# A linear-attention and mixer kernel: VectorE's small product of u's and w's rows moves ahead of three products of the second unit

## Chip, cores and metric

The kernel runs on one core of a Trainium2 chip. A core has TensorE (PE, matrix products into PSUM; a weight load is shown as PEld), VectorE (DVE), ScalarE (ACT), GpSimd (POOL) and SyncE (SP), which run side by side, each through its own queue in order, and wait for one another by semaphores. Data comes from HBM into SBUF by DMAs that SP, ACT and GpSimd issue. The metric is device time in microseconds (us); the median of several runs is compared.

## What is computed

Two stages follow each other. The first is a linear attention with a decayed state (4 batches, 8 heads, 768 steps, 48 columns a head):

```python
for t in range(S):
    kt, vt, rt = (k[:, :, t], v[:, :, t], r[:, :, t])
    cur = np.einsum('bhd,bhe->bhde', u[None] * kt, vt)
    y[:, :, t] = np.einsum('bhd,bhde->bhe', rt, state + cur)
    state = w[None, :, :, None] * state + np.einsum('bhd,bhe->bhde', kt, vt)
```

The second is a mixer on x, which is y with the heads side by side (4 x 768 x 384):

```python
xt = x.transpose(0, 2, 1)
h = np.maximum(xt @ w_tok1, 0.0) @ w_tok2
u = x + h.transpose(0, 2, 1)
h2 = np.maximum(u @ w_ch1, 0.0) @ w_ch2
return (u + h2).astype(np.float32)
```

## The kernel before

The attention is worked in blocks of steps: scores between the steps of a block, masked to the causal half, and a state that carries what lies before the block. Powers of w are kept as tables (exp of iota times ln w); k and r are multiplied by them, turned by PE so that the columns lie on the partitions, and multiplied with each other to give scores (`at_ps`). The own step's term (u times k times r, summed over a head) comes apart from that: the product `pr` of the turned k and r goes through PE against `u_blk`, a matrix with u times w on its block diagonal, since the exponents of the two tables add up to -1 for the own step.

The first batch takes its 768 steps as three units of 256 (`pair_unit`): partition p holds steps 2p and 2p+1, so each of k and r is scaled in two steps (j = 0, 1). The other batches take 128 steps at a time (`unit`). The mixer of a batch follows its attention and overlaps the next batch's.

Nothing here is ordered by a scheduler at run time. The program makes 889 tasks, each with the tasks that it depends on, and emits them in the order of the list `ORDER`; `keep_in_program_order` holds every engine's instructions to that. The choice of engine of a flexible task (`flex`) is the list `ENGINES`, that of buffers the list `BUFS`. Two tasks on one engine therefore run in the order in which `ORDER` has them, and a task that waits holds up everything behind it on its engine.

The tasks around the change, by their number in `ORDER`:

- 126, 127: first unit's two products of k with its tables (GpSimd, VectorE). 130, 131: its two products of r (both VectorE). 128 and 132 turn them on PE; 129 and 133 copy the results to SBUF (`ka`, `rkb`) on ScalarE.
- 154, 155: second unit's products of k (both VectorE). 158, 159: its products of r (VectorE, GpSimd). 156 and 160 turn them on PE (`tk_ps`, `tr_ps`); 157 and 161 copy. 182: third unit's first product of k (GpSimd).
- 47: the small product `u_heads *= w_heads` on 8 partitions and 128 columns; both are parts of the tile `wp`, which the table of the same name fills later. It waits for the DMAs of u's and w's rows (issued by ACT at the start) and is on VectorE.
- 48: PE turns its result (`ud_ps`). 50: VectorE copies it onto the diagonal of `u_blk`. 139, 142: first unit's scores on PE; 140, 141, 143, 144: VectorE masks them (`AT`).
- 134: VectorE's product `pr` of the first unit; 135: PE's sum of it against `u_blk` (`ad_ps`).
- 43: GpSimd's `wGm` (a table of the state's decay). 61, 64, 67: GpSimd's loads of v for the three units. 119, 120: its loads of w_tok.
- 869 to 888: matmuls on zeros that keep PE warm (`kv_ps<-warm`).

VectorE's queue here is 127, 130, 131, 154, 155, 158, 47, 134, 50, 140, 143, 141, 144. PE's is 128, 132, 156, 48, 139, 142, 160, 135, with warming matmuls between. GpSimd's is 61, 64, 67, 159, 182, 43, 183, 119, 120.

Of the kernel before, what the change touches and what calls it, by code (L numbers as in the profile page):

```python
# [20 lines left out]
ORDER = [  # L21
    9, 57, 26, 3, 46, 0, 886, 884, 880, 1, 17, 8, 4, 6, 27, 24, 56, 59, 18, 19, 20, 10, 60, 2, 62, 878, 887,
    45, 42, 11, 12, 13, 21, 25, 14, 22, 63, 49, 877, 5, 29, 58, 65, 7, 16, 28, 23, 33, 126, 66, 31, 69, 888,
    34, 127, 869, 15, 68, 36, 32, 130, 131, 883, 30, 128, 61, 154, 129, 885, 132, 64, 133, 879, 155, 882,
    158, 67, 47, 134, 159, 156, 876, 48, 157, 50, 139, 140, 40, 142, 143, 160, 161, 182, 43, 141, 144, 135,
    873, 51, 52, 881, 170, 172, 872, 874, 71, 70, 38, 870, 162, 875, 186, 136, 35, 871, 145, 183, 184, 146,
    163, 119, 187, 171, 120, 73, 167, 138, 74, 147, 148, 185, 188, 150, 164, 149, 137, 173, 190, 191, 165,
    189, 151, 168, 121, 169, 166, 192, 152, 198, 199, 174, 175, 153, 195, 176, 197, 308, 178, 177, 179, 181,
# [1200 lines left out]
```

## Time and profile before

| what | us |
|---|---|
| three runs | 160.78, 165.18, 166.24 |
| median of them | 165.18 |
| profiled execution | 161.76 |
| its span, first to last instruction | 160.0 |
| loads of v, GpSimd: issue to landing, median of three | 8.2 |
| loads of k and r for the first batch's units, SP: issue to landing, median | 4.7 and 6.1 |

The profile is one execution; times in it count from the start of the span. Busy time of an engine leaves out register, semaphore and DMA-issuing instructions. "[1.23 <-DVE wp L274]" behind a row means that the engine sat idle for 1.23 us before it and that VectorE's write to wp ended that. All operations are recorded by one helper and so have the line L274; they are told apart by the tiles, out<-in. Recorded spans on GpSimd are rough.

### The profile page before, as it was taken

How to read it: one execution, taken by the hardware profiler on the slowest of the kernel's cores; microseconds unless marked ns; L12 is line 12 of the kernel's file. 1: busy time of each engine (PE TensorE's matmuls, PEld its weight loads, DVE VectorE, ACT ScalarE, POOL GpSimd, SP SyncE). 2: the span in 40 equal slices, each digit the busy share in tenths (PEclk: the TensorE clock that was granted, in tenths of full speed). 3: DMA queues.
4: the chain of work that ended last, by engine and by line, in shares of the span. 5: the costliest groups of instructions: out<-in, count | busy, mean ns of one | idle time of the engine just before them, and what ended most of it. 6: DMA issues, size and time to landing. Idle time of an engine off the chain costs nothing.

```text
span 160.0 us, 3938 instructions
## 1 busy us (share of the span) xinstructions
PE 153.3 (96%) x1563; PEld 102.3 (64%) x1564; DVE 116.1 (73%) x237; ACT 68.5 (43%) x154; POOL 77.7 (49%) x103
## 2 busy tenths in 40 slices
PE   6978999999999999999999999989999999999992
PEld 1455776777776666667767665656667556666662
DVE  5499895699697976697899888657998382644332
ACT  3874666649667263132852041168504202450100
POOL 7798569200899816955765543965906000000000
PEclk9999999999999999999999999999999999999999
DMA  4999999999999929999899899999794057010423
GB/s 124 263 243 183 165 195 222 222 205 181 197 196 214 200 74 217 211 228 212 153 196 222 157 200 187 178 210 209 148 189 103 4 158 185 2 49 4 147 74 123
DMA packets 88005, 26.60 MB, mean 166 GB/s; under 512 B 82738, under 2 KB 87092, under 8 KB 87988
## 3 DMA queue, kind: packets, MB, share of 16 engines
q1 hardware_dynamic: 82512, 22.52, 71.0%
q0 software_dynamic: 5280, 3.74, 15.2%
q8 instruction: 12, 0.20, 0.5%
q10 hardware_dynamic: 196, 0.11, 0.2%
q14 instruction: 5, 0.04, 0.1%
HBM read 20.46 MB, written 4.72 MB: 157 GB/s over the span
## 4 chain that ended last, share of the span: by engine, by line
PE 85%; DVE 6%; ACT 2%; DMA 2%; SPq 1%; issue 1%; DVEq 0%; ACTq 0%
PE h_ps L274 35%; PE z_ps L274 25%; PE y_ps L274 5%; PE kv_ps L274 5%; PE at_ps L274 4%; PE hT_ps L274 4%; DMA out_dram<-osb 2%; DVE kr L274 2%; PE hx_ps L274 2%; DVE wp L274 2%; SPq L274 1%; PE tr_ps L274 1%; PE w_ps L274 1%; PE trk L274 1%; DVE osb L274 1%
## 5 line engine op out<-in xcount | busy, mean ns | idle before, releaser
L274 PE MATMUL h_ps<-wch,zr 128*128 128x384 bf16 (+1 forms) x300 | 52.8, 320 | 0.0
L274 PE MATMUL z_ps<-uT,wch 128*128 128x384 bf16 x288 | 50.8, 326 | 0.2 <-DVE osb L274 0.2
L274 ACT ACTIVATE zr<-z_ps 128x384 bf16<-128x384 f32 x63 | 28.6, 492 | 41.4 <-PE z_ps L274 41.2
L274 PEld LDWEIGHTS <-wch 128*128 128x128 bf16 x288 | 31.5, 114 | 13.1 <-issue 0.7
L274 PEld LDWEIGHTS <-zr 128*128 128x128 bf16 x300 | 27.8, 98 | 16.1
L274 DVE TENSOR_SCALAR zr<-z_ps 128x384 bf16<-128x384 f32 x33 | 17.5, 553 | 10.1 <-PE z_ps L274 8.8
L274 DVE TENSOR_TENSOR AT<-at_ps,mask 128x512 bf16<-128x512 f32 x36 | 23.1, 682 | 0.9 <-PE at_ps L274 0.8
L274 DVE TENSOR_TENSOR osb<-u_sb,h_ps 128x384 f32<-128x384 bf16 (+1 forms) x19 | 10.1, 531 | 11.6 <-PE h_ps L274 7.8
L274 POOL TENSOR_TENSOR kr<-kt,wnat 128x384 bf16<-128x384 f32 x13 | 13.0, 1008 | 11.0 <-DMA kt<-in_k_dram 11.0
L274 POOL TENSOR_TENSOR yd<-vb,adg 128x384 f32<-128x384 bf16 x15 | 12.3, 829 | 8.0 <-ACT vb L274 7.4
L274 PEld LDWEIGHTS <-kr 128*128 128x128 bf16 (+1 forms) x196 | 12.4, 101 | 4.8 <-issue 2.0
L274 ACT CAST S<-kv_ps 48x192 bf16<-48x192 f32 (+1 forms) x26 | 8.8, 338 | 8.8 <-PE kv_ps L274 7.1
L274 POOL TENSOR_TENSOR rku<-ku,rt 128x384 f32<-128x384 f32 x10 | 10.2, 1019 | 3.1 <-DVE ku L274 1.8
L274 PEld LDWEIGHTS <-wtok 128*128 128x128 bf16 x84 | 8.0, 98 | 5.2
L274 POOL TENSOR_TENSOR ku<-kt,u_bc 128x384 f32<-128x384 f32 x10 | 9.9, 999 | 2.6 <-DVE rku L274 2.6
L274 DVE TENSOR_TENSOR x_b<-y_ps,yd 128x384 bf16<-128x384 f32 x18 | 9.7, 552 | 2.0 <-PE y_ps L274 1.8
L274 DVE TENSOR_TENSOR u_sb<-x_b,hT_ps 128x384 bf16<-128x384 bf16 x18 | 8.9, 550 | 2.7 <-PE hT_ps L274 2.6
L274 POOL TENSOR_TENSOR kr<-rt,wp 128x384 bf16<-128x384 f32 x9 | 9.1, 1009 | 3.5 <-ACT wp L274 3.5
L274 ACT CAST vb<-vt 128x384 bf16<-128x384 f32 x14 | 7.1, 514 | 6.2 <-DMA vt<-in_v_dram 6.1
L274 PE MATMUL kv_ps<-warm 128*128 128x512 bf16 x19 | 7.8, 521 | 1.5 <-DVE warm L274 1.5
L274 PE MATMUL h_ps<-x_b,wtok 128*128 128x384 bf16 x48 | 8.6, 326 | 0.0
L274 DVE TENSOR_REDUCE adg<-rku 128x8 f32<-128x384 f32 x12 | 6.6, 546 | 2.5 <-POOL rku L274 2.5
(108 smaller groups left out, 191.1 us busy)
## 6 DMA issues: line engine op xcount, KB each, us to landing
out_dram<-osb SPq DMA_DIRECT2D x23, 192.0 KB, 2.2
kt<-in_k_dram SPq DMA_DIRECT2D x18, 192.0 KB, 6.4
vt<-in_v_dram SPq DMA_DIRECT2D x18, 192.0 KB, 4.3
rt<-in_r_dram SPq DMA_DIRECT2D x12, 192.0 KB, 3.7
wch<-in_moe_w_ch_dram POOLq DMA_DIRECT2D x4, 384.0 KB, 7.5
zr<-in_k_dram SPq DMA_DIRECT2D x3, 384.0 KB, 4.7
zr<-in_r_dram SPq DMA_DIRECT2D x3, 384.0 KB, 6.1
win<-in_r_dram SPq DMA_DIRECT2D x3, 384.0 KB
```

The lines of the kernel that those rows point to most:

```text
L274: return lambda *args, **kw: tc.keep_in_program_order(f(*args, **kw))
```

## The change

Task 47 is emitted behind task 131, the second product of r of the first unit, and no longer behind task 158 (between 67 and 134). Since 130, 131, 154, 155 and 158 are VectorE's, as 47 is, its queue becomes 127, 130, 131, 47, 154, 155, 158, 134, 50 and so on. The tasks between the old and the new place on the other engines (883, 30, 128, 61, 129, 885, 132, 64, 133, 879, 882, 67 and the like) keep their order among themselves. The rest of the diff is the list's lines set anew.

```diff
-    34, 127, 869, 15, 68, 36, 32, 130, 131, 883, 30, 128, 61, 154, 129, 885, 132, 64, 133, 879, 155, 882,
-    158, 67, 47, 134, 159, 156, 876, 48, 157, 50, 139, 140, 40, 142, 143, 160, 161, 182, 43, 141, 144, 135,
+    34, 127, 869, 15, 68, 36, 32, 130, 131, 47, 883, 30, 128, 61, 154, 129, 885, 132, 64, 133, 879, 155,
+    882, 158, 67, 134, 159, 156, 876, 48, 157, 50, 139, 140, 40, 142, 143, 160, 161, 182, 43, 141, 144, 135,
```

The task itself is not touched:

```python
t_uw = flex({"DVE": "tiny_dve", "POOL": "tiny_pool"},
            lambda on: engine_of[on].tensor_mul(u_heads, u_heads, w_heads), [t_urows, t_wh])
```

## The prediction

> **What bounds the kernel now.** I read the page's head first, then busy time by stretch.
>
> ```profile
> span 160.0 us, 3938 instructions
> PE 153.3 (96%) x1563; PEld 102.3 (64%) x1564; DVE 116.1 (73%) x237; ACT 68.5 (43%) x154; POOL 77.7 (49%) x103
> 0.00:25.50 25.50, 22.35 (x328) 13.58 (x330) 20.91 (x49) 15.51 (x29) 19.61 (x40) 1.00 1.22 195
> 25.50:101.00 75.50, 75.46 (x797) 51.72 (x798) 61.14 (x123) 35.43 (x84) 43.84 (x49) 1.00 1.03 196
> 101.00:109.40 8.40, 7.77 (x56) 5.20 (x55) 4.94 (x10) 4.01 (x10) 5.97 (x7) 1.00 1.09 180
> 109.40:160.00 50.60, 47.71 (x386) 31.80 (x385) 29.08 (x57) 13.56 (x32) 8.27 (x9) 1.00 0.42 104
> ```
>
> In the stretches the columns are length, then busy us of PE, weight loads, VectorE, ScalarE, GpSimd, the granted TensorE clock (1.00 throughout), DMA share and GB/s. TensorE bounds the kernel: from 25.50 to 101.00 it lacks 0.04 us. Its idle time that an edit at the start can reach is in the first 25.5 us, and the small product is there. So the next view is the chain of waits around it (start, us, what).
>
> ```profile
> 6.72 2.99 DVE kr L274 x6
> 9.71 2.65 DVE wp L274
> 12.37 0.04 issue
> 12.41 0.38 PE ud_ps L274 x2
> ```
>
> The product of 8x128 numbers (wp<-wp) stands on the chain with 2.65 us behind VectorE's six products kr. The timeline of VectorE (start, duration) says that this is not its own cost:
>
> ```profile
> 7.20 0.64 DVE L274 TENSOR_TENSOR kr<-zr,wpair 128x384 bf16<-128x384 f32 x1
> 7.76 0.55 DVE L274 TENSOR_TENSOR kr<-zr,wpair 128x384 bf16<-128x384 f32 x1
> 8.23 0.54 DVE L274 TENSOR_TENSOR kr<-zr,u_sb 128x384 bf16<-128x384 f32 x1
> 8.70 0.55 DVE L274 TENSOR_TENSOR kr<-zr,u_sb 128x384 bf16<-128x384 f32 x1
> 9.17 0.54 DVE L274 TENSOR_TENSOR kr<-zr,wpair 128x384 bf16<-128x384 f32 x1
> 9.64 2.72 DVE L274 TENSOR_TENSOR wp<-wp 8x128 f32<-8x128 f32 x1
> 12.29 0.67 DVE L274 TENSOR_TENSOR pr<-tr_ps,ka 128x1024 bf16<-128x1024 bf16 x1
> 12.89 0.35 DVE L274 CAST u_blk<-ud_ps 64x4 bf16<-64x4 f32 x2
> 13.27 3.32 DVE L274 TENSOR_TENSOR AT<-at_ps,u_sb 128x512 bf16<-128x512 f32 x5
> ```
>
> A product with three times the columns takes 0.54 us, this one 2.72. GpSimd's timeline shows what it stood beside, and the last two rows show the same thing once more, later:
>
> ```profile
> 6.98 0.45 POOL L274 TENSOR_SCALAR_AFFINE_SELECT mask<-mask 128x128 f32<-128x128 f32 x1
> 7.39 2.85 POOL L274 DMA_DIRECT2D zr<-in_v_dram  x3
> 10.23 1.03 POOL L274 TENSOR_TENSOR kr<-zr,wpair 128x384 bf16<-128x384 f32 x1
> 11.19 1.01 POOL L274 TENSOR_TENSOR kr<-zr,u_sb 128x384 bf16<-128x384 f32 x1
> 12.20 0.85 POOL L274 TENSOR_TENSOR wGm<-bm,wG 128x384 f32<-128x384 f32 x1
> 59.67 1.07 POOL L274 TENSOR_TENSOR kr<-rt,wp 128x384 bf16<-128x384 f32 x1 [3.54 <-ACT wp L274]
> 59.80 1.35 DVE L274 TENSOR_TENSOR kr<-kt,wnat 128x384 bf16<-128x384 f32 x1
> ```
>
> VectorE's product at 59.80 ends at 61.15, 0.41 us after GpSimd's ends at 60.74: it was held and then streamed. The one at 7.20 took 0.64 and ends at 7.84, 0.41 after the mask's select ends at 7.43. The small product ends at 12.36, 0.15 us after GpSimd's second kr ends at 12.20: a third of the columns, about a third of 0.41. All three read both inputs from SBUF while GpSimd reads SBUF. So 12.36 is the hold's end, and the price of the small product by itself is near 0.2 us.
>
> The Trainium skill, page SBUF — State Buffer, section Who interferes with whom, says this: a VectorE instruction with two SBUF inputs and a GpSimd instruction that reads SBUF exclude each other, and the one that starts first has the port for its whole length. The three holds agree.
>
> **When GpSimd takes the port decides the change.** By recorded starts the small product (9.64) would have been ahead of GpSimd's kr (10.23), yet it did not run between 9.71, when the product before it ended, and 10.23. So the claim lies ahead of the recorded start. What does GpSimd's kr wait for? The second unit's r, whose load shows as (timeline, then DMA issues: KB, us to landing)
>
> ```profile
> 3.05 1.28 SPq L274 DMA_DIRECT2D zr<-in_r_dram  x1
> zr<-in_r_dram SPq DMA_DIRECT2D x1, 384.0 KB, 6.1
> ```
>
> and so lands at 3.05 + 6.1 = 9.15. VectorE's sixth product reads the same load and starts at 9.17. The claim therefore lies between 9.15 and 9.71, while GpSimd's record still shows the generation of descriptors for v (7.39 to 10.23).
>
> The skill's page GPSIMD Engine Reference, section 2.1 Instruction dispatch, gives a reason: the eight cores do not wait for each other between instructions, so a core with no share in the generation goes on to the next one. By that rule the claim comes right at 9.15 and task 158 inherits the hold (the sum below, +0.2 us); by recorded starts alone the hold would be gone (the first rival, -1.2 us). The trace agrees with the rule as far as 9.71 to 10.23 goes.
>
> **The change, part by part.** No instruction, wait or DMA is added or removed. Task 47 is emitted behind task 131 (the product at 7.76) and ahead of 154, 155, 158 (8.23, 8.70, 9.17). On POOL's, SP's and ACT's queues nothing moves; in the order it also passes GpSimd's loads of v (64, 67), copies of ACT and matmuls of PE, which stand in other queues.
>
> Small product: it takes the place at 8.23, inside the generation of descriptors, in which four products (7.76 to 9.17) ran unheld at 0.54 to 0.55. Price 0.15 to 0.47 us (the remainder after 12.20, the spacing of the products); I take 0.2, being nearer the small one. It waits for the rows of u; that wait is over by 9.2 in this trace (21 ns in VectorE's sequencer), and no view shows how long before:
>
> ```profile
> L274 DVEq EVENT_SEMAPHORE  x1: 21/21/21, 9.2 to 9.2; - x1
> ```
>
> If it were not over at 8.23, at most 0.95 us would be lost, with 154, 155 and 158 queued behind it.
>
> Tasks 154, 155, 158 start 0.2 us later: 8.43, 8.90, 9.37. The first two are ahead of 9.15. PE turns their results at 10.36 (tk_ps, below), 0.9 us after 155 ends at 9.45, so the 0.2 us is covered by PE's earlier work. Task 158 at 9.37 is now behind GpSimd's claim, if that comes between 9.15 and 9.37. Then it inherits the hold to 12.20, plus 0.41: it ends at 12.61.
>
> PE gets the diagonal of u (ud_ps) early. What is late next there:
>
> ```profile
> 10.36 0.61 PE L274 MATMUL tk_ps<-ident,kr 128*128 128x128 bf16 x8
> 10.80 0.38 PE L274 MATMUL kv_ps<-warm 128*128 128x512 bf16 x1
> 12.41 0.38 PE L274 MATMUL ud_ps<-ident_f,wp 8*128 8x8 f32 x2 [1.23 <-DVE wp L274]
> 12.72 0.64 PE L274 MATMUL at_ps<-rkb,ka 48*64 48x128 bf16 x32
> 13.30 0.62 PE L274 MATMUL tr_ps<-ident,kr 128*128 128x128 bf16 x8
> 15.42 0.26 PEld L274 LDWEIGHTS <-ka 48*64 48x64 bf16 x16 [0.23 <-DVE AT L274]
> 9.98 1.01 ACT L274 COPY rkb<-tr_ps 128x1024 bf16<-128x1024 bf16 x1 [0.27 <-PE tr_ps L274]
> ```
>
> rkb is ready at 10.99 and the warming matmul ends at 11.18, so ud_ps runs from 11.2 and the scores at_ps from 11.5, 1.2 us earlier. The second unit's tr_ps waits for 158: about 12.65 instead of 13.30.
>
> VectorE then has pr, u_blk and the masks AT, in that order, all behind 158. pr starts 0.07 us before its forerunner's end, so at 12.54 instead of 12.29, and AT 0.98 later at most, at 13.52 instead of 13.27; with ud_ps long done some 0.05 to 0.1 of it may be saved. So VectorE is 0.2 us later, and the second unit's scores at 15.42 wait for AT to free PSUM, so PE is too. **Sum: +0.2 us**; the 1.2 us won on PE are idle time moved behind the scores. GpSimd's wGm at 12.20 is held 0.41 instead of 0.15 us by VectorE's 158, and with it what is queued behind it: the table's reader on VectorE and the loads of w_tok, with PE's first use of them:
>
> ```profile
> 19.25 0.57 DVE L274 TENSOR_TENSOR kv_ps<-kv_ps,wGm 128x384 f32<-128x384 f32 x1 [0.45 <-PE kv_ps L274]
> 13.95 1.45 POOL L274 DMA_DIRECT2D wtok<-in_moe_w_tok_dram  x2
> wtok<-in_moe_w_tok_dram POOLq DMA_DIRECT2D x2, 384.0 KB, 9.8
> 25.50 0.76 PE h_ps L274 x4
> ```
>
> The table has 6 us to spare, and w_tok, at 13.95 + 9.8 = 23.75, has 1.7 us, so this costs nothing.
>
> The profiled execution took 161.76 us (span 160.0), 3.42 below the median 165.18 of the three runs. It becomes 162.0; at the median 165.4. The forecast is stated at the median.
>
> **The rivals.** Hold gone: VectorE's 158 still comes ahead of GpSimd's claim (claim after 9.37, or r landing 0.2 us later than here). Then nothing waits for the port: 158 ends at 9.9, pr runs at 9.9 with ka, u_blk follows ud_ps at 11.5, AT starts at 12.0. The scores' 1.2 us reach the end, since PE is full from 25.5 on: 160.5, at the median 164.0. For it: the window 9.37 to 9.71 is the larger part of 9.15 to 9.71. Against it: what would release the claim, the landing at 9.15, lies before 9.37.
>
> Held at the new place, on the other side: it is the generation of descriptors that holds the small product, not the next kr. Then it waits from 8.31 to 12.36 at its new place, and 154, 155, 158 run behind it from 12.29 at 0.47 each. tk_ps starts at 13.3 instead of 10.36, then 0.82 us to the warming matmul's end and 0.31 for ud_ps, so at_ps comes at 14.4 instead of 12.72: +1.7, 163.5, at the median 166.9. It decides if the hold begins with anything before 8.31. Against it: four products in the same generation were not held.
>
> No effect of its own: the change does nothing measurable, since the hold falls on the same place in most executions, or 155 is caught as well (claim before 8.90, which needs r 0.25 us earlier; two held products cost 0.47 more, +0.7).
>
> **How the numbers follow.** Hold inherited by 158: 0.50. Hold gone: 0.28. Held at the new place: 0.12. No effect of its own: 0.10. No case reaches 2% (3.3 us of 165.18, about what a measurement of this kernel can tell from no change); but three runs of one kernel lie between 160.78 and 166.24. So faster 0.13 comes from about half of the hold that is gone (1.2 us, with runs at the lower end), slower 0.07 from about half of the one held at the new place (1.7 us, with runs at the upper end), same 0.80. Range: 160.78 less 1.2 to 166.24 plus 0.2, so 159.6 to 166.5; the held case at the upper end is left out. The likeliest case alone: 161.0 to 166.5.
>
> **What would show it.** wp<-wp at 8.2 with about 0.25 us: first step right; with several us: second rival. The last kr<-zr,wpair before pr at some 3 us, ending at 12.6: the hold inherited; at 0.54: gone. at_ps of the first unit at 11.5, tr_ps of the second at 12.65 (inherited) or 12.1 (gone), the first AT at 13.5 or 12.0. The forecast is wrong if the start comes out over 1.5 us earlier or later, or if PE gets idle time behind 25.5 us.

## The result, and the profile after

| | before | changed |
|---|---|---|
| runs, us | 160.78, 161.45, 165.12, 165.18, 166.24, 166.70 | 158.86, 158.95, 159.33, 159.38, 159.84, 160.15 |
| median | 165.15 | 159.36 |
| profiled execution (span) | 161.76 (160.0) | 159.33 (157.6) |

The forecast was 165.4, with 159.6 as its low end; the median is 159.36. The ratio that is given, 0.9897 with a 95% interval of 0.9861 to 0.9932, compares the changed kernel with before's shorter executions alone, so it is a gain of 1.0%; by the medians the gain is 3.5%, since before's executions near 166 have no counterpart any more. Both gains have to be explained.

Page head and busy time by stretch of the changed kernel (length, then busy us of PE, weight loads, VectorE, ScalarE, GpSimd, then granted clock, DMA share, GB/s):

```profile
span 157.6 us, 3939 instructions
PE 152.7 (97%) x1564; PEld 102.4 (65%) x1564; DVE 114.5 (73%) x237; ACT 68.3 (43%) x154; POOL 78.0 (49%) x103
0.00:25.50 25.50, 23.71 (x349) 14.57 (x350) 18.89 (x49) 16.73 (x32) 21.01 (x41) 1.00 1.22 196
25.50:101.00 75.50, 75.28 (x786) 51.73 (x786) 62.81 (x125) 34.70 (x83) 44.84 (x51) 1.00 1.09 199
101.00:109.40 8.40, 8.40 (x62) 5.94 (x60) 5.92 (x13) 5.62 (x15) 5.51 (x6) 1.00 1.26 226
```

PE's busy time in the first 25.5 us is 23.71 instead of 22.35: 1.36 us of idle time are gone there. From 25.5 to 101.0 it lacks 0.22 instead of 0.04, and from 101.0 to 109.4 it has none left, where it lacked 0.63. VectorE's timeline at the place of the change, then PE's:

```profile
8.23 0.27 DVE L274 TENSOR_TENSOR wp<-wp 8x128 f32<-8x128 f32 x1
8.44 1.01 DVE L274 TENSOR_TENSOR kr<-zr,u_sb 128x384 bf16<-128x384 f32 x2
9.37 0.54 DVE L274 TENSOR_TENSOR kr<-zr,wpair 128x384 bf16<-128x384 f32 x1
11.01 0.69 DVE L274 TENSOR_TENSOR pr<-tr_ps,ka 128x1024 bf16<-128x1024 bf16 x1 [1.10 <-ACT rkb L274]
11.61 0.35 DVE L274 CAST u_blk<-ud_ps 64x4 bf16<-64x4 f32 x2
11.99 3.13 DVE L274 TENSOR_TENSOR AT<-at_ps,u_sb 128x512 bf16<-128x512 f32 x5
...
10.19 0.61 PE L274 MATMUL tk_ps<-ident,kr 128*128 128x128 bf16 x8
10.95 0.38 PE L274 MATMUL ud_ps<-ident_f,wp 8*128 8x8 f32 x2
11.26 0.64 PE L274 MATMUL at_ps<-rkb,ka 48*64 48x128 bf16 x32
23.97 0.83 PE L274 MATMUL h_ps<-x_b,wtok 128*128 128x384 bf16 x4
```

The small product takes 0.27 us. The sixth product, task 158, takes 0.54 us at 9.37: it does not wait, though GpSimd's side is what it was (10.23 and 11.19 for its two products kr):

```profile
10.23 1.03 POOL L274 TENSOR_TENSOR kr<-zr,wpair 128x384 bf16<-128x384 f32 x1
12.16 0.83 POOL L274 TENSOR_TENSOR wGm<-bm,wG 128x384 f32<-128x384 f32 x1
```

So nobody inherits the hold of 2.72 us in this execution. ud_ps starts at 10.95 instead of 12.41, 1.46 us earlier, and this distance is kept up to h_ps (25.43 on the timeline of before, now 23.97). Of the 1.46 us, 0.17 come from tk_ps, which stands at 10.19 and stood at 10.36; that is chance, as the start of tk_ps moves from execution to execution (9.26 to 10.59 in the twenty profiles of this case). Behind it some of it is given back, in part at a short wait of PE's:

```profile
25.72 0.50 PE L274 MATMUL y_ps<-zr,AT 64*128 64x48 bf16 x26 [0.24 <-issue]
26.48 0.40 PE L274 MATMUL trk<-ident,kr 128*128 128x128 bf16 x4
...
27.55 0.40 PE L274 MATMUL trk<-ident,kr 128*128 128x128 bf16 x4
```

The last row is the second one's forerunner in the profile of before: 1.07 us of the 1.46 are left here. The rest of the span's 2.4 us comes late, at the output. VectorE's writes of the last results but a few, before and then changed:

```profile
103.72 0.56 DVE L274 TENSOR_TENSOR osb<-u_sb,h_ps 128x384 f32<-128x384 bf16 x1 [0.91 <-DMA out_dram<-osb]
108.72 0.56 DVE L274 TENSOR_TENSOR osb<-u_sb,h_ps 128x384 f32<-128x384 bf16 x1 [2.31 <-DMA out_dram<-osb]
...
101.43 0.55 DVE L274 TENSOR_TENSOR osb<-u_sb,h_ps 128x384 f32<-128x384 bf16 x1
106.10 0.55 DVE L274 TENSOR_TENSOR osb<-u_sb,h_ps 128x384 f32<-128x384 bf16 x1 [1.79 <-DMA out_dram<-osb]
```

Before, both writes wait for an output buffer whose store is not done; after, the first does not and the second waits 0.5 us less. The second is 2.62 us earlier, so some 1.5 us beyond the 1.07 that PE had kept. PE's own distance grows there from 1.30 us (kv_ps at 101.97, now 100.67) to 2.42 (y_ps at 111.76, now 109.34); a wait of 0.40 us for VectorE's AT and one of 0.15 for its osb are gone. Of the 2.4 us a part belongs to the execution that was profiled: the shorter executions of the kernel before have a median of 161.0 (34 of them, see below), and the profiled one took 161.76, while the profiled 159.33 of the changed kernel lies at its median.

### The profile page after: what moved, and what is told of

It reads as the page before. It is cut to its first block, busy times and chain, and to the rows that moved or that the text cites. A ratio compares the mean times of both kernels' runs of the same rounds, so it can differ in the third digit from the quotient of the medians.

```text
span 157.6 us, 3939 instructions
## 1 busy us (share of the span) xinstructions
PE 152.7 (97%) x1564; PEld 102.4 (65%) x1564; DVE 114.5 (73%) x237; ACT 68.3 (43%) x154; POOL 78.0 (49%) x103
## 4 chain that ended last, share of the span: by engine, by line
PE 95%; DVE 1%; ACT 1%; issue 1%; DVEq 0%; ACTq 0%
PE h_ps L274 36%; PE z_ps L274 30%; PE kv_ps L274 7%; PE y_ps L274 6%; PE at_ps L274 4%; PE hT_ps L274 4%; PE tr_ps L274 2%; PE hx_ps L274 2%; PE tk_ps L274 1%; PE w_ps L274 1%; PE trk L274 1%; PE ad_ps L274 1%; PE u_ps L274 1%; DVE pr L274 0%; ACT rkb L274 0%
## 5 line engine op out<-in xcount | busy, mean ns | idle before, releaser
L274 PEld LDWEIGHTS <-kr 128*128 128x128 bf16 (+1 forms) x196 | 12.4, 101 | 4.6 <-issue 1.8
```

What stands on the lines that cost most here:

```text
L274: return lambda *args, **kw: tc.keep_in_program_order(f(*args, **kw))
```

## The experiments

All kernels that follow compute the whole result. The copies named `scr` are added work that nobody uses; the rows that two kernels add to the small product are unused too. Task numbers from 889 on are the added tasks.

Runs of the kernel before stood beside all of them. With those above there are 82: 34 lie from 160.35 to 162.19, 48 from 165.02 to 170.74, and none between. These are the lower and the upper group in what follows, and the second gain is about them.

### Is it the port, and is it this product's data?

The first kernel puts a copy of the small product, on other data, at the old place; the second does the same with one input in PSUM.

```diff
+    scr = const.tile([8, 128], f32, name="scr")
+    once("DVE", "dup", lambda: dve.tensor_mul(scr, ident_f[0:8, :], ident_f[0:8, :]), [t_idf])
-    882, 158, 67, 134, 159, 156, 876, 48, 157, 50, 139, 140, 40, 142, 143, 160, 161, 182, 43, 141, 144, 135,
+    882, 158, 889, 67, 134, 159, 156, 876, 48, 157, 50, 139, 140, 40, 142, 143, 160, 161, 182, 43, 141, 144, 135,
```

> The changed kernel with a copy of the small product (8x128, both inputs from SBUF, ready since 5 us, result used by nobody) at the old place, behind VectorE's sixth product kr. Port theory (GpSimd's next two products hold the port from about 9.9 to 12.2): the copy starts at 9.84 and ends at 12.3 to 12.4, 2.5 us long; pr moves from 11.0 to 12.3, the first AT from 12.0 to 13.0 or later, and the time goes back by 1.0 to 1.5 us at least, into the spread of the kernel before (160.8 to 166.7). Rival (at its old place the small product waited for its own rows of u and w, not for the port): the copy takes 0.3 us inside VectorE's idle time before pr, and the time stays at 159.4.

```diff
-    once("DVE", "dup", lambda: dve.tensor_mul(scr, ident_f[0:8, :], ident_f[0:8, :]), [t_idf])
+    once("DVE", "dup", lambda: dve.tensor_mul(scr, ident_f[0:8, :], early["L"]["tr"][0:8, 0, 0, :]), [t_idf, early["t_tr"]])
```

> As late_copy, but one of the copy's two inputs is read from PSUM (a corner of the turned r, ready at 9.94). Port theory: only one SBUF input is left, so it is not held: 0.2 to 0.4 us long, done by 10.4 while VectorE would be idle, time 159.4 as the changed kernel. Rival (any instruction at this place is held, whatever it reads): it ends at 12.3 as in late_copy, time 160.8 or more.

VectorE's timeline of the first, then GpSimd's last product before its next loads, and PE; then VectorE's timeline of the second:

```profile
9.84 4.24 DVE L274 TENSOR_TENSOR scr<-ident_f 8x128 f32<-8x128 f32 x1
12.93 1.00 POOL L274 TENSOR_TENSOR kr<-zr,u_sb 128x384 bf16<-128x384 f32 x1
14.73 0.61 PE L274 MATMUL tr_ps<-ident,kr 128*128 128x128 bf16 x8 [2.90 <-DVE pr L274]
...
11.02 0.28 DVE L274 TENSOR_TENSOR scr<-ident_f,tr_ps 8x128 f32<-8x128 f32 x1 [1.11 <-ACT rkb L274]
```

The copy is held for 4.24 us, to 14.08: not to the end of GpSimd's second product, as the small product was, but past its fourth, which ends at 13.93. The four runs took 160.5 to 164.84 (median 163.53). With one input from PSUM the same instruction takes 0.28 us at 11.02 (later than expected, as it waits for ScalarE's rkb), while GpSimd's first product ends and its second begins (11.19), and the median is 159.97. So the hold is real, the data of u and w have no part in it, and it goes with the second SBUF input; the comparison is not quite like with like, since the second copy runs 1.18 us later than the first, inside GpSimd's products and not ahead of them. The length of the hold is not fixed: it seems to last until GpSimd's chain of instructions that read SBUF has a gap.

### Where does the second group of run times come from?

If the hold ends at the first gap in GpSimd's chain, a chain without a gap makes it 1.7 us longer. In the profile of before GpSimd's second kr ended at 12.20 and wGm began at 12.20, where the others overlap by 0.04 to 0.07. The likely reason is ScalarE's table wG, which was ready at 12.12. The next kernel is the one before with task 40, that table, moved up behind task 30 on ScalarE.

```diff
-    34, 127, 869, 15, 68, 36, 32, 130, 131, 883, 30, 128, 61, 154, 129, 885, 132, 64, 133, 879, 155, 882,
-    158, 67, 47, 134, 159, 156, 876, 48, 157, 50, 139, 140, 40, 142, 143, 160, 161, 182, 43, 141, 144, 135,
+    34, 127, 869, 15, 68, 36, 32, 130, 131, 883, 30, 40, 128, 61, 154, 129, 885, 132, 64, 133, 879, 155, 882,
+    158, 67, 47, 134, 159, 156, 876, 48, 157, 50, 139, 140, 142, 143, 160, 161, 182, 43, 141, 144, 135,
```

> The kernel before, with ScalarE's small table wG made right behind ln_wd (at 8 us) instead of at 11.9, so that GpSimd's third product wGm never waits for it. Theory of the two lengths (the hold ends at 12.2 when GpSimd pauses for wG ahead of wGm, and at 13.9, behind the fourth product, when it does not; the longer one idles TensorE so long that its granted clock falls): always the long hold, small product 4.2 us long in the profile, granted clock about 0.99 over the run, every run at 164.5 to 168. Rival (the slow executions of the kernel before are something else): both kinds as before, 160.4 to 169.

```profile
9.64 4.44 DVE L274 TENSOR_TENSOR wp<-wp 8x128 f32<-8x128 f32 x1
14.14 0.59 PE L274 MATMUL ud_ps<-ident_f,wp 8*128 8x8 f32 x2 [2.85 <-DVE wp L274]
14.00:16.00 2.00, 1.86 (x38) 1.67 (x39) 1.69 (x6) 0.00 (x0) 1.31 (x2) 0.50 1.54 158
16.00:18.00 2.00, 2.00 (x17) 1.32 (x15) 1.83 (x4) 1.01 (x1) 0.00 (x0) 0.50 1.54 150
```

These are VectorE's and PE's timelines and busy time by stretch. The small product now takes 4.44 us, PE is idle for 2.85 us before ud_ps, and from 14 to 18 us the granted clock is 0.50. All four runs lie between 165.69 and 167.29 (ratio 1.0341, 1.0282 to 1.0401): a table that comes earlier makes the kernel slower, and only the upper group is left.

The opposite: a gap is put into GpSimd's chain for certain, by moving the first load of w_tok (task 119) between its third kr (182) and wGm (43).

```diff
-    158, 67, 47, 134, 159, 156, 876, 48, 157, 50, 139, 140, 40, 142, 143, 160, 161, 182, 43, 141, 144, 135,
+    158, 67, 47, 134, 159, 156, 876, 48, 157, 50, 139, 140, 40, 142, 143, 160, 161, 182, 119, 43, 141, 144, 135,
...
-    163, 119, 187, 171, 120,
+    163, 187, 171, 120,
```

> The kernel before, with GpSimd's generation of descriptors for w_tok's first load (0.89 us, reads no SBUF tensor) between its second product kr and wGm. If the generation lets go of the port: the small product always ends at 12.36, no long hold, all runs at 160.4 to 162. If GpSimd's next product claims the port during the generation, as it seems to at 9.6: the small product is held through wGm and the fourth product to 14.8, runs at 165 to 169, or both kinds.

The hold is 2.72 us and ends at 12.36; the load stands at 12.13 on GpSimd's timeline. VectorE's and GpSimd's rows:

```profile
9.64 2.72 DVE L274 TENSOR_TENSOR wp<-wp 8x128 f32<-8x128 f32 x1
12.13 0.89 POOL L274 DMA_DIRECT2D wtok<-in_moe_w_tok_dram  x1
```

Nine of ten runs lie between 160.78 and 162.89, one at 165.27 (ratio 1.0065, 1.0023 to 1.0106). So one edit of GpSimd's chain leaves only the upper group and another all but removes it: the two groups are two lengths of one hold. One thing is left over: four of the nine runs, from 162.32 to 162.89, have a granted clock of 0.989, where the lower group of before has 1.00. The profile is of the run at 160.78, so how long the hold was in those four is not known.

### Is it the lateness, or the output buffers?

A rival says that the two groups come from a late start, which brings some loads and stores into an unlucky order. The changed kernel with six more warming matmuls ahead of ud_ps is late without a hold:

```diff
-NWARM = 20
+NWARM = 26
-    158, 67, 134, 159, 156, 876, 48,
+    158, 67, 134, 159, 156, 876, 889, 890, 891, 892, 893, 894, 48,
```

> The changed kernel with six more warming matmuls on PE ahead of ud_ps, some 1.4 us; VectorE's and GpSimd's products stay as in the changed kernel. Theory A (what the early place gives is a start of TensorE that is earlier by 1.46 us, and the further 1 us of the profile and the spread of the kernel before come from how the start lies against the later stores and loads): the time goes back to that of the kernel before, 160.8 to 166.7 with a wide spread. Theory B (the spread of the kernel before has another cause than the late start): 159.4 + 1.4 = 160.8, with a spread below 1.5 us.

PE's timeline:

```profile
11.80 0.38 PE L274 MATMUL ud_ps<-ident_f,wp 8*128 8x8 f32 x2
```

ud_ps starts 0.85 us later than in the changed kernel, not the 1.4 us that were meant and not as late as before's 12.41, and eleven runs give 160.18 to 161.5, median 161.0 (ratio 0.9976, 0.9941 to 1.0012). The time is about that of before's lower group, and the upper group does not appear. By itself this tests only part of the lateness; the rest is answered by the profiles of the kernels before_32_rows and before_fourth_osb below, in which ud_ps starts at 12.41 or 12.42 and the time is of the lower group (160.42 and 160.45). So a start at 12.4 does not make the upper group; the longer hold does, with the still later start and the lost clock behind it.

A fourth output buffer takes away the waits near 104 and 109 us; the first of these kernels is the one before with one entry of the buffers' list changed, the second the same in the changed kernel.

```diff
     'osb': [
-    0, 1, 2, 0, 1, 0, 1, 1, 1, 1, 2, 0, 0, 2, 1, 2, 0, 2, 0, 2, 0, 1, 2, 0, 1,
+    0, 1, 2, 0, 1, 0, 1, 1, 1, 1, 2, 3, 0, 2, 1, 2, 0, 2, 0, 2, 0, 1, 2, 0, 1,
```

> The kernel before, with a fourth output buffer for the one result whose write at 108.7 waited 2.3 us for a store. Theory W (this wait is what the later 1 us and the slow executions of the kernel before come from): fast runs faster by 0.5 to 1.2 us, 159.6 to 160.3, and all runs within 1.5 us. Rival (the wait at 108.7 is a follower of a late queue on SyncE, which delays other things too): 160.8 to 166.7 as before, with the wait gone from its place.

> The changed kernel with the fourth output buffer of before_fourth_osb. In the changed kernel the write still waits 1.8 us for its store, but PE is busy throughout 101 to 109, so if that reading is right there is nothing to gain: 158.9 to 160.2. If the wait does reach PE: up to 0.7 us faster.

The one before gives 160.45 to 161.11 four times and 165.11 to 169.82 four times: both groups stay, so the output buffers do not make them (ratio 0.9951, 0.9902 to 1.0). The changed one gives 159.63 (ratio 0.9906, 0.9849 to 0.9963), no more than the change alone. To the kernel before, which is late, the wait at the output is worth 0.8 us by the ratio, with an interval that reaches zero; to the changed kernel, nothing that shows.

### Why did task 158 not inherit the hold?

By the forecast's reasoning an instruction that starts after r's landing at 9.15 comes behind GpSimd's claim. These kernels bring the sixth product to later times, with one and with two copies of the small product behind task 47:

```diff
-    34, 127, 869, 15, 68, 36, 32, 130, 131, 47, 883,
+    34, 127, 869, 15, 68, 36, 32, 130, 131, 47, 889, 883,
```

> The changed kernel with one copy of the small product right behind the early one: VectorE's sixth product kr starts at 9.57 instead of 9.37. The claim of GpSimd lies between 9.37 (sixth product not held there) and 9.64 (small product held there). If GpSimd claims the port once its last generation of descriptors has begun (9.35, plus some 0.1 us): the sixth product is held, 2.9 to 4.6 us long, ends at 12.6 or 14.3, time 161 or more. If it claims at 9.6 or later: 0.54 us long, time 159.5.

> The changed kernel with two copies behind the early small product: the sixth product kr starts at 9.77, past 9.64 where the small product was held in the kernel before. Port theory: held, ends 0.41 us behind GpSimd's second or fourth product, at 12.6 or 14.3; time 161 to 168 with the spread of the kernel before. Rival (only the small product's form, 8 partitions, is held here): 0.54 us long, time 159.8.

The sixth product of the one and of the other:

```profile
9.57 0.54 DVE L274 TENSOR_TENSOR kr<-zr,wpair 128x384 bf16<-128x384 f32 x1
9.88 0.54 DVE L274 TENSOR_TENSOR kr<-zr,wpair 128x384 bf16<-128x384 f32 x1
```

Neither is held, though the second ends at 10.42, past the recorded start of GpSimd's product (it came 0.1 us later than meant, as the two copies took 0.58 us together). In the second, GpSimd's next product starts at 11.25 and not at 11.19, which fits GpSimd having waited there and not VectorE. Medians are 159.83 (0.9925, 0.9875 to 0.9975) and 160.02 (0.9943, 0.9914 to 0.9971). Three kernels then changed what stands there: a second copy of the sixth product behind it, a copy of the small one with 128 partitions, and the real small product between the fifth and the sixth.

```diff
+    once("DVE", "dup", lambda: dve.tensor_mul(scr[:, :, 0:D], loaded[0, 2, 1][:, :, 0:D], h3(wp2[:, 0, :])), [t_load[0, 2, 1], t_wp2[0]])
...
+    once("DVE", "dup", lambda: dve.tensor_mul(scr, ident_f, ident_f), [t_idf])
...
-    34, 127, 869, 15, 68, 36, 32, 130, 131, 47, 883, 30, 128, 61, 154, 129, 885, 132, 64, 133, 879, 155,
+    34, 127, 869, 15, 68, 36, 32, 130, 131, 883, 30, 128, 61, 154, 129, 885, 132, 64, 133, 879, 155, 47,
```

> The changed kernel with a second copy of the sixth product itself (128x384, same inputs, into a scratch tile) behind it, at 9.84, where the small copy was held to 14.1. Theory K (VectorE keeps the port while products of one form follow each other, and GpSimd, waiting since some point between 9.15 and 9.64, gets it as soon as the form changes): not held, 0.54 us, time 159.4 to 160.5. Theory F (the hold at 9.6 to 10.2 strikes only instructions on 8 partitions): not held either, same time. Theory P as predicted (GpSimd owns the port from about 9.6 on): held, ends at 12.6 or 14.3, time 161 to 168.

> As late_copy, but the small copy has 128 partitions instead of 8 (128x128 f32, both inputs from SBUF), at 9.84. Theory K (a change of form gives the port away): held, ends at 12.3 or 14.0, time 160.5 to 166. Theory F (only 8 partitions are struck): 0.27 us long, time 159.4 to 160.2.

> The changed kernel with the small product between VectorE's fifth and sixth product kr instead of behind the third: it starts at 9.17, the sixth at 9.37. Theory K: the small one ends the run of like products at 9.25, so it is held if GpSimd claims before 9.25, or the sixth behind it is held if it claims before 9.45: one of the two 2.9 us or longer, time 161 to 168. If GpSimd claims later than 9.45, or by theory F with a claim later than 9.25: neither is held, 0.27 and 0.54 us, time 159.4.

The copies' rows in the first two:

```profile
9.84 0.54 DVE L274 TENSOR_TENSOR scr<-zr,wpair 128x384 bf16<-128x384 f32 x1
9.85 0.27 DVE L274 TENSOR_TENSOR scr<-ident_f 128x128 f32<-128x128 f32 x1
```

Nothing is held in the profile of any of the three (in the last the small product starts at 9.17, the sixth at 9.37); medians 160.28, 159.44 and 159.58. So at one place, 9.84, a copy on 8 partitions was held and one on 128 was not. Is it the width, and where is the bound?

```diff
+    scr = const.tile([128, 128], f32, name="scr")
+    once("DVE", "dup", lambda: dve.tensor_mul(scr[64:72, :], ident_f[64:72, :], ident_f[64:72, :]), [t_idf])
```

> The changed kernel with an unused copy of a small product behind task 158, again with 8 partitions and 128 columns, but on partitions 64 to 71 and not 0 to 7. Theory N (the number of partitions decides: an instruction with few partitions is struck wherever they lie): it is held from about 9.84 to 12.2 or 13.9, so 2.4 to 4.2 us long, and PE's ud_ps stays near 10.95 while tr_ps comes late. Theory L (the place decides: what uses only the low partitions is struck): it takes 0.27 us at about 9.84, and the time stays within 1 us of the change's 159.4.

The other three have 0:64, 0:32 and 0:16 for 64:72.

> The same with 64 partitions, 0 to 63, and 128 columns. Theory N, if the bound lies at or above 64 partitions, and theory L, if the low half counts as low: held 2.4 to 4.2 us. If the bound lies lower: 0.27 us at about 9.84. Either way it narrows the bound between 8, which was held, and 128, which was not.

> The same with 32 partitions, 0 to 31, and 128 columns. Held 2.4 to 4.2 us if the bound lies at or above 32 partitions; 0.27 us at about 9.84 if it lies between 8 and 32.

> The changed kernel with an unused copy of a small product behind task 158, on 16 partitions, 0 to 15. Held from about 9.84 for 2.4 to 4.2 us if the bound lies at or above 16 partitions; 0.27 us if it lies between 8 and 16. 8 partitions were held and 32 were not.

The copy in the four, in this order:

```profile
9.94 4.15 DVE L274 TENSOR_TENSOR scr<-ident_f 8x128 f32<-8x128 f32 x1
9.84 0.27 DVE L274 TENSOR_TENSOR scr<-ident_f 64x128 f32<-64x128 f32 x1
9.84 0.27 DVE L274 TENSOR_TENSOR scr<-ident_f 32x128 f32<-32x128 f32 x1
9.84 4.24 DVE L274 TENSOR_TENSOR scr<-ident_f 16x128 f32<-16x128 f32 x1
```

One run each: 164.11, 159.41, 158.93 and 168.26. This looked like a bound between 16 and 32 partitions, wherever they lie. If it were the whole cause, the kernel before would lose its hold when its small product is made wider at its old place, with no change of the order. This was run with 32 rows and with all 128:

```diff
-    t_wh1 = once("DVE", "memset_s", lambda: dve.memset(w_heads, 1.0))
-    t_uh0 = once("DVE", "memset_s", lambda: dve.memset(u_heads, 0.0))
+    t_wh1 = once("DVE", "memset_s", lambda: dve.memset(wp[0:32, 2, 0:2 * P], 1.0))
+    t_uh0 = once("DVE", "memset_s", lambda: dve.memset(wp[0:32, 2, 2 * P:4 * P], 0.0))
-                lambda on: engine_of[on].tensor_mul(u_heads, u_heads, w_heads), [t_urows, t_wh])
+                lambda on: engine_of[on].tensor_mul(wp[0:32, 2, 2 * P:4 * P], wp[0:32, 2, 2 * P:4 * P], wp[0:32, 2, 0:2 * P]), [t_urows, t_wh])
```

> The kernel before, with its order untouched: the small product stays at its old place behind task 158, but it and the two memsets of its operands cover 32 partitions and not 8 (the rows added are unused). Theory N (only an instruction with few partitions is struck, the bound lying between 8 and 32): the product takes 0.27 us at about 9.64, ud_ps comes near 10.95, no run lies above 162, and the median is within 1 us of the changed kernel's 159.4. Rival (the place in the order matters, whatever the width, here with the second operand's rows that arrive by DMA): it is held to 12.2 or 13.9 as before, and the runs keep their two groups near 161 and 166.

> The kernel before, its order untouched, with the small product and the two memsets of its operands on all 128 partitions (120 rows unused). At 32 rows the product was held at this place, while an unused copy with 32 rows at 9.84 in the changed kernel was not. Theory N, corrected (the number of partitions decides, but the bound isn't the same everywhere): the product takes 0.27 us at about 9.64, ud_ps comes near 11.2, no run lies above 162.5 and the median is within 1 us of the changed kernel's 159.4. Theory W (at its old place the product is struck whatever its width; what counts lies in the order, for instance that the product ahead of it starts right at the landing of r): held to 12.2 or 13.9, ud_ps at 12.4 or later, runs near 161 and near 166 as before.

VectorE's timelines of the two, behind each row GpSimd's wGm and PE's ud_ps, and for the second busy time by stretch:

```profile
9.68 2.69 DVE L274 TENSOR_TENSOR wp<-wp 32x128 f32<-32x128 f32 x1
12.56 0.83 POOL L274 TENSOR_TENSOR wGm<-bm,wG 128x384 f32<-128x384 f32 x1 [0.35 <-ACT wG L274]
12.42 0.38 PE L274 MATMUL ud_ps<-ident_f,wp 8*128 8x8 f32 x2 [0.88 <-DVE wp L274]
...
9.63 4.44 DVE L274 TENSOR_TENSOR wp<-wp 128x128 f32<-128x128 f32 x1
12.13 0.84 POOL L274 TENSOR_TENSOR wGm<-bm,wG 128x384 f32<-128x384 f32 x1
14.13 0.38 PE L274 MATMUL ud_ps<-ident_f,wp 8*128 8x8 f32 x2 [3.48 <-DVE wp L274]
14.00:16.00 2.00, 1.87 (x51) 1.51 (x51) 1.96 (x6) 0.32 (x1) 1.31 (x2) 0.96 1.53 159
16.00:18.00 2.00, 2.00 (x4) 0.60 (x3) 1.47 (x3) 0.93 (x2) 0.00 (x0) 0.50 1.54 149
18.00:20.00 2.00, 2.00 (x20) 0.84 (x20) 1.11 (x2) 1.25 (x3) 0.00 (x0) 0.50 1.42 185
20.00:25.00 5.00, 4.94 (x95) 3.67 (x94) 2.83 (x7) 2.15 (x5) 2.61 (x3) 0.73 1.22 207
```

Both are held, and both kernels keep both groups: seven runs from 160.36 to 161.65 and three from 166.61 to 167.09 with 32 rows (ratio 1.0, 0.9965 to 1.0035), and 161.39 beside three at 165.28 to 165.35 with 128. So width alone does not decide, and the explanation by width falls for the kernel before.

The two profiles happen to show one execution of each group; beside the rows of the product, which cost nothing themselves, the length of the hold is what differs. Where GpSimd waits 0.35 us for ScalarE's wG, the hold ends at 12.37; where it does not wait, at 14.07, and ud_ps comes 1.71 us later (14.13, against 12.42 in the first). From 14 to 25 us PE then loses, by the granted clock, 0.04 x 2 + 0.50 x 4 + 0.27 x 5 = 3.4 us of full speed. Together 5.1 us; the spans are 158.7 and 163.6, 4.9 apart.

Why one order gives both lengths can be followed one step further back. In the same two profiles, PE's turning of the second unit's k and ScalarE's wG, which stands behind the copy of its result:

```profile
10.59 0.74 PE L274 MATMUL tk_ps<-ident,kr 128*128 128x128 bf16 x8
12.28 0.21 ACT L274 ACTIVATE wG<-lnwd 128x4 f32<-128x4 f32 x1
...
9.83 0.61 PE L274 MATMUL tk_ps<-ident,kr 128*128 128x128 bf16 x8
11.41 0.23 ACT L274 ACTIVATE wG<-lnwd 128x4 f32<-128x4 f32 x1
```

Eight such matmuls take 1.06 us at 7.60 in both profiles and 0.61 or 0.62 us later, and the moment at which they get faster differs from execution to execution. With it tk_ps, the copy and wG move, and wG is ready before or after GpSimd's second product ends, near 12.2. Among the profiles with a held product whose order of GpSimd and of the table is untouched, wG was ready at 11.64 to 11.96 in the four with a hold of over 4 us and at 12.12 to 12.49 in the three with one of 2.7 us. So the executions in which PE gets fast early are those with the long hold. What sets that moment is not shown; the granted clock reads 1.00 all the time there.

## Why the prediction was wrong, step by step

**The small product at 8.23 is free.** Right: 0.27 us, and the products behind it start 0.2 us later (8.44). The rival in which the descriptors' generation holds it is out. So is the rival of no effect, by the ratio's interval.

**154 and 155 are covered.** Right: tk_ps starts at 10.19, no later than the 10.36 of before. That it is even earlier is chance, as said above.

**"Task 158 at 9.37 is now behind GpSimd's claim."** This is the step that failed. It was one inference from one instruction: the small product waited from 9.71 on, GpSimd's wait for r ended at 9.15, so whatever starts after 9.15 waits. 158 ran in 0.54 us at 9.37, and even at 9.57 and 9.88: it ended at 9.91, not at 12.61, and the +0.2 us of the sum, which rested on that wait, came out as a start that is 1.46 us earlier. The premise that GpSimd takes the port ahead of its recorded start still fits, as copies at 9.84 were held while GpSimd's product is recorded from 10.23 on; that the first instruction behind the landing is the one caught does not.

**What then follows, the rival of a hold that is gone.** It had 0.28 and described the changed kernel well: scores at 11.5, found at 11.26; u_blk at 11.5, found at 11.61; the first AT at 12.0, found at 11.99; a gain of 1.2 us at the start, found as 1.46. One detail differs: pr was to run at 9.9 and ran at 11.01, since it waits for rkb. Nothing comes of it, as AT needs at_ps anyway.

**"The scores' 1.2 us reach the end, since PE is full from 25.5 on."** Nearly: 0.4 is given back by trk, 0.24 of it at the wait before y_ps, and the waits for output buffers near 104 and 109 us get shorter, so that 2.4 us reach the end of the profiled execution. pe_late prices the start from the other side: 0.85 us of lateness cost 1.64 us of median (161.0 against 159.36, run beside different executions of before; by the two ratios 0.8%, some 1.3 us). So a us at the start may be worth more than a us here, but the two intervals leave room for one that is worth just that. The rival's term was right in sign and too small.

**"Three runs of one kernel lie between 160.78 and 166.24."** The second error, and the larger one in us. The forecast took this for spread and carried the profiled execution's 3.42 us below the median over to the changed kernel, in every case. It is not spread but the hold itself, at two lengths, and the lost clock behind the longer one. A change that removes the hold removes the upper group: of the 61 runs of the eleven kernels in whose profile no product is held there (the changed one, pe_late and nine more), none is above 161.77. In the upper group itself no unedited execution of before was profiled; what it looks like is taken from before_table_early and before_128_rows. The rival's 164.0 should have been its own 160.5 for the profiled execution, with nothing added.

**The loads and the table cost nothing.** Right: wGm stands at 12.16 (12.20 before) and h_ps came 1.46 us earlier without a wait for w_tok.

**What stays open.** What decides at which product GpSimd gets the port. At its old place the small product was held at each of three widths; behind 158 in the changed kernel copies on 8 and 16 partitions were held and those on 32, 64 and 128 were not; no kr of the second unit was ever held. A race at each hand-over between two VectorE instructions would fit all of these, but nothing here measures it. The widths of 16, 32 and 64 partitions behind 158 rest on one run each, and chance is a rival to width there: of late_copy's own four runs one took 160.5, so the same copy may go unheld, or be held for less time, in another execution.

## What to carry to other kernels

A small instruction on VectorE with two SBUF inputs can cost as much as GpSimd's products up to the next gap (4.44 us here): put it ahead of GpSimd's chain, or give it one input in PSUM, and look for the gap in the chain at which the hold would end. Run times that fall into two groups are not noise to be added to a forecast; ask which wait has two lengths and what decides between them, and price the change in each group. And a hold seen on one instruction says little on which other one would be caught: give the case that nobody inherits it at least the same chance, unless a second instruction was seen to be held there.

## What the runs showed of the hardware that was not expected

The hold spans several GpSimd instructions. The Trainium skill, page SBUF — State Buffer, section Who interferes with whom, says that the one that issues first has the shared port for the whole instruction; here VectorE's product was kept for the length of two (2.72 us) or four (4.24 and 4.44 us) GpSimd products run one behind the other, and a gap for descriptor generation let it go at 12.36 (before_load_between). With one input in PSUM it was not kept, which agrees with that section.

The clock falls after less idle time of PE than thought: 2.85, 2.90 and 3.48 us of waiting (before_table_early, late_copy, before_128_rows) were followed by a granted clock of 0.50 to 0.61 over 2 us and more, and in before_table_early the clock falls inside the wait already (0.73 on average from 13.50 to 14.00, where PE's next matmul stands at 14.14); 1.23 us (the profile of before) were followed by none. The row of late_copy, in the columns of the stretches:

```profile
16.00:18.00 2.00, 2.00 (x20) 0.64 (x19) 1.69 (x4) 1.74 (x4) 0.00 (x0) 0.61 1.54 149
```

The Trainium skill, page TensorE: Matmul & The Clock Gate, Part 1, has the clock halved after at least one idle window of about 3.4 us. The halved clock agrees with the runs; the length does not, since a wait of 2.85 us was enough here.

A table that ScalarE delivered earlier left only the longer executions (165.69 to 167.29 in before_table_early), since GpSimd's wait for it had been the gap at which VectorE got the port back.
